# Two chunks of attention per PE run, half loads of the first k and q, dummy matmuls in early gaps

## The chip, the cores and the metric

The kernel runs on one core of one Trainium2 chip. The metric is the device time of one execution in microseconds (us). Before the change the median of three runs is 304.57 us (304.15 to 305.27). In the text PE is TensorE (matmuls), ACT is ScalarE, DVE is VectorE, POOL is GpSimd, and SP is SyncE, whose queue issues all DMA transfers.

## What is computed

Sliding-window causal attention (8 batches, 8 heads, 576 tokens, head size 64, window 64), and then a feed-forward layer with a squared ReLU on all 4608 tokens (512 to 2048 to 512 features):

```python
scores = scale * np.matmul(q, k.transpose(0, 1, 3, 2))
rel = pos[:, None] - pos[None, :]
mask = (rel >= 0) & (rel < window)          # window = 64
attn = softmax(np.where(mask, scores, -1e9))
x = np.matmul(attn, v)                      # per token, heads side by side: (4608, 512)
h = np.maximum(x @ w_in, 0.0)               # (4608, 2048)
out = (h * h) @ w_out                       # (4608, 512)
```

## The kernel before

**Tiling.** The tokens are cut into 36 chunks of 128, and four chunks make a group (9 groups). Groups 0 to 6 and 8 take the first 512 tokens of a batch each; group 7 (LEFT) gathers the last 64 tokens of all eight batches. A chunk's attention is 16 score matmuls (4 head pairs, 2 blocks of 64 queries, 2 heads; contraction over 64 rows), two exps on ACT, two masks on DVE, two halves of values (8 matmuls of 64 columns each) and two normalisations on DVE. The four chunks of a group then share the feed-forward layer.

**Order.** There is no loop that sets the order. A long string, PROGRAM (L16), names one step after another, and each step issues its instructions; every engine runs its own in that order. A step's name, its numbers and, after @, its engine are to be read so:

- lk, lq, dk, dq, dv, li, lo: loads of k and q of a whole group, of k, q or v of one chunk, of a quarter of w_in and w_out (SP).
- ck, cq, ek, eq, cv, ci, co: casts to fp16. cs, cn: copies that shift v by 64 tokens (POOL).
- Tk, Tq: transposes of a group's k or q on PE into PSUM; tk, tq copy them out. Kk, Kq: the same by a DMA transpose (SP). X, x: a chunk's attention output transposed on PE and copied; xx: two chunks by a DMA transpose.
- S, E, M, V, N: scores, exps (E chunk.head), masks, values (V chunk.half) and norms.
- U, R, Q: up projection of one chunk by a quarter of w_in (16 matmuls of 128 columns), its relu on ACT and its square. u, r, s: the same for a whole group and 128 features (4 matmuls of 512 columns).
- O, Z, z: down projection of group 0 as it stands, the copy from PSUM, and the store.
- p, sa, ta, va, vc, vz: down projection of groups 1 to 8 by seven products of half size (Strassen's scheme in Winograd's form): p group.product.half is 8 matmuls of 256 columns, sa and ta are sums on DVE of h and of w_out, va and vc combine products on DVE (one on ACT), vz stores a quarter.
- W: dummy matmuls of zeros at the very start.

Group 0 works in chunks (U, O), groups 1 to 3 use U or u, and from group 1's products (p1.1.0) on, the up blocks of the next group, the products of this one and the attention of the one after are interleaved on PE.

**Buffers.** [...]two for up blocks (ps_up, L151), two for products (ps_out), four for attention (ps_att, L153: transposes, scores and values). A chunk's scores take two banks, its values two. hrelu (hrp, L148) has four buffers. k, q and weight loads share two tags of two buffers each (kq_a and kq_b, L140).

**Squares.** L157 and L158 say on which engine each square runs: all of the groups' on ACT, and of the chunks' some on DVE.

Of the kernel before, what the change touches and what calls it, by code (L numbers as in the profile page):

```python
# [16 lines left out]
    lk0 lq0 dv0 ck0.0@A ck0.1@D ck0.2@P dv2 ck0.3@D W14 Tk0.0 Tk0.1 tk0.0@A dv1 tk0.1@D cq0.2@A  # L17
    cq0.3@P cq0.0@D li0 cq0.1@A Tq0.1 Tq0.0 cv0@A tq0.1@D tq0.0@A cn0@P cv2@A S0 li1 S1 cn2@P
    E0.0 E0.1 cv1@D cs2@P E1.0 M0.0 S2 cs1@P E1.1 M0.1 M1.0 E2.0 cn1@P V0.1 dv3 V0.0 M1.1 E2.1
    N0.1 V1.0 V1.1 N0.0 ci0.0@A ci0.1@P li2 N1.0 S3 N1.1 X0 E3.0 M2.0 X1 E3.1 x0@D x1@D U0.0@u  # L20
    M3.0 ci1.0@A ci1.1@P M3.1 li3 U1.0@u M2.1 R0.0 V2.1 cv3@A V2.0 N2.1 U1.1@o Q0.0 cs3@P N2.0
    R1.0 U0.1@o R1.1 lo1 Q1.0 X2 Q1.1 V3.0 R0.1 V3.1 ci2.0@P x2@D ci2.1@A N3.0 U2.0@u N3.1
    U1.2@u Q0.1 lk1 R2.0 X3 Q2.0 U2.1@o x3@D ci3.0@P ci3.1@A U3.0@u R2.1 R1.2 U0.3@o lo0 Q2.1
    R3.0 Q1.2 U3.1@o R0.3 co1.0@P co1.1@D Q3.0 U0.2@u Q0.3 R3.1 U3.2@u lq1 R0.2 Q3.1 U1.3@o R3.2
    Q0.2 ck1.0@P ck1.1@A U2.3@o ck1.2@D ck1.3@P R1.3 Q3.2 Tk1.0 Q1.3 lo2 Tk1.1 tk1.0@D R2.3
    U3.3@o tk1.1@A co0.0@P U2.2@u co0.1@D Q2.3 R3.3 O0.0.0 R2.2 lo3 Q3.3 O0.0.1 Q2.2 cq1.0@A
    cq1.1@P cq1.2@D O0.1.0 cq1.3@D Tq1.0 Tq1.1 dv4 tq1.0@A O0.1.1 tq1.1@D co2.0@A co2.1@P dv5
    ta1.1@D S6 S4 ta1.0@D E6.0 O0.1.2 dv6 E4.0 ta3.0@D E4.1 O0.0.2 M4.0 E6.1 co3.0@P lk2 M4.1
    co3.1@A S5 M6.0 S7 M6.1 E5.0 cv4@P O0.0.3 ta2.0@D E7.0 E7.1 M5.0 cn4@P V4.0 O0.1.3 M7.0 E5.1
    cv5@P dv7 M7.1 Z0.0 V4.1 M5.1 Z0.1 cs5@P O0.2.0 N4.0 lq2 cv6@P N4.1 V5.0 V5.1 ta2.1@D cn5@P  # L30
    O0.2.1 N5.0 cn6@P O0.2.2 N5.1 cs6@P ta3.1@D O0.3.0 ck2.0@A ck2.1@P z0.0 ck2.2@A ck2.3@D V6.1
    xx5 ta4.0@D V6.0 Tk2.0 cv7@P N6.1 O0.2.3 tk2.0@A N6.0 cs7@P z0.1 O0.3.1 ta4.1@D Z0.2 dv8
    V7.1 O0.3.2 N7.1 cq2.0@A cq2.1@P cq2.2@D V7.0 z0.2 cq2.3@A O0.3.3 N7.0 dv9 Tq2.0 Z0.3 Tq2.1
    tq2.0@D U4.0@u tq2.1@A z0.3 U4.3@u xx7 R4.0 Tk2.1 Q4.0 cv8@P R4.3 tk2.1@D U4.1@u dv10 Q4.3
    cn8@P R4.1 U4.2@u dv11 Q4.1 cv9@P S9 R4.2 U5.2@u cn9@P E9.0 dk12 Q4.2 E9.1 cs9@P S8 M9.0
    R5.2 U5.1@u M9.1 E8.0 dk13 Q5.2 V9.0 E8.1 S10 R5.1 M8.0 U6.3@u cv10@P M8.1 E10.0 dk14 N9.0
    E10.1 V8.0 cs10@P M10.0 Q5.1 V9.1 V8.1 M10.1 cv11@P R6.3 dk15 U5.3@u N8.0 cn10@P Q6.3 N9.1
    V10.0 R5.3 cs11@P V10.1 N8.1 dq12 U5.0@u N10.0 Q5.3 ek12@P S11 N10.1 R5.0 ek13@P xx9 U7.0@u
    E11.0 E11.1 M11.0 ek14@P Q5.0 M11.1 dq13 R7.0 U7.3@u Q7.0 ek15@P V11.1 R7.3 dq14 V11.0 N11.1
    U6.1@u Q7.3 N11.0 eq12@P p1.1.0 R6.1 xx11 U6.0@u Q6.1 U6.2@u R6.0 dq15 p1.1.1 Q6.0 eq13@P  # L40
# [36 lines left out]
    N25.1 E26.1 dl30 M26.0 p4.6.0 ek39@P s5.8 M26.1 r5.9 p4.6.1 dl31 s5.9 eq28@P u5.10 va4.1 Kk9
    p4.7.0 r5.10 u5.11 s5.10 eq29@P V25.0 r5.11 dv36 S27 N25.0 p4.7.1 eq30@P E27.0 E27.1 V26.0
    M27.0 xx25 p4.5.0 s5.11 N26.0 eq31@P M27.1 V26.1 u5.4 va4.2 Kq7 N26.1 V27.1 r5.4 u5.5 N27.1
    s5.4 V27.0 p4.5.1 r5.5 N27.0 dv37 cv36@P s5.5 u5.7 sa5.1.0@D xx27 u5.6 va4.3 r5.7 sa5.2.0@D  # L80
    p4.4.0 s5.7 r5.6 vc4.3 dk40 p4.4.1 s5.6 p4.3.0 vc4.2 vz4.3 u5.13 vz4.2 cv37@P u5.12 dk41
    r5.13 p4.3.1 s5.13 r5.12 dk42 p5.1.0 sa5.3.0@D s5.12 u5.14 sa5.3.1@D ek40@P dk43 sa5.4.0@D
    u5.15 r5.14 vc4.1 dv38 S28 s5.14 p5.1.1 r5.15 E28.0 ek41@P u6.1 vz4.1 E28.1 M28.0 s5.15 dv39
    S29 M28.1 r6.1 ek42@P u6.0 sa5.1.1@D E29.0 E29.1 dv42 V28.1 sa5.2.1@D p5.2.0 r6.0 ek43@P
    M29.0 s6.1 p5.2.1 M29.1 Kk10 s6.0 sa5.4.1@D cv38@P va5.0 u6.2 N28.1 u6.8 vc5.0 r6.2 dv43
    V28.0 s6.2 p5.6.0 cv39@P N28.0 r6.8 u6.3 vz5.0 s6.8 cv42@P dv40 u6.9 r6.3 p5.6.1 s6.3 dv41
    r6.9 V29.1 va5.1 S30 s6.9 u6.10 E30.0 N29.1 dk32 E30.1 cv43@P V29.0 M30.0 S31 r6.10 N29.0
    u6.11 E31.0 dk33 M30.1 E31.1 p5.7.0 M31.0 r6.11 M31.1 cv40@P xx29 s6.10 p5.7.1 s6.11 u6.4
    va5.2 cv41@P dk34 V31.0 r6.4 V30.0 N31.0 u6.5 ek32@P s6.4 N30.0 dk35 p5.5.0 r6.5 ek33@P
# [25 lines left out]
def kernel(  # L115
# [38 lines left out]

    NV = 8
    LEFT = B - 1
    SQUARE = "AAAA"  # L157
    SQUARE4 = ('ADDA', 'AADA')  # L158
    FQ = DFF // 4

# [550 lines left out]
```

The softmax here doesn't subtract the row's maximum and nothing guards it: scores larger than these inputs give would overflow.

## Time and profile before

| what | before |
|---|---|
| median of 3 runs | 304.57 us |
| profiled execution | 303.55 us |
| its span, first to last instruction | 301.8 us |
| PE busy | 287.6 us |
| ACT busy | 220.7 us |
| DVE busy | 187.1 us |
| POOL busy | 107.8 us |
| first matmul of U0.0 | 19.31 us |
| first matmul of p1.1.0 | 74.93 us |
| start of the last matmul's tail (p8.3.1) | 297.8 us |

The time of an execution holds 1.75 us around the span. An engine's busy time is the sum of its instructions. Matmuls are pipelined, so that one begins before the one before it has ended; the distance from one start to the next is what a block costs, and the busy share alone doesn't tell how well PE is used. Steps were put to times by counting: PE's matmuls come in the order of the string, and the number of each step is known.

### The profile page before, as it was taken

Reading aid. Unit: us, or ns where it says so; the run is one execution under the profiler, and the core shown is the slowest. Engines: PE = TensorE matmul, PEld = TensorE weight load, DVE = VectorE, ACT = ScalarE, POOL = GpSimd, SP = SyncE. Lnnn points to the kernel's source line nnn. Section 1 sums busy time; section 2 is a strip of 40 time slices with the busy share of each in tenths; the row PEclk is TensorE's granted clock in tenths of the full one; section 3 lists DMA queues with packets and bytes.
Section 4 is the critical chain, followed back from the end, with each engine's and each line's share of the span. In section 5 each row is a group of like instructions: output and inputs, shape, how many; then the busy total and the mean of one; then the engine's idle time right before and its main releaser. Section 6 shows DMA issues by size and latency. Waiting matters only on the chain.

```text
span 301.8 us, 7861 instructions
## 1 busy us (share of the span) xinstructions
PE 287.6 (95%) x3198; PEld 196.4 (65%) x3198; DVE 187.1 (62%) x395; ACT 220.7 (73%) x386; POOL 107.8 (36%) x161
## 2 busy tenths in 40 slices
PE   7489997999999999999999999999999999999994
PEld 2379953698865666666656666656667566666683
DVE  3676679868559666755855585555766296524453
ACT  2879975699799679578886785688865887877710
POOL 3444229556246408522832662133440350000000
PEclk9759999999999999999999999999999999999999
DMA  7999999999999999999999978999979905210323
GB/s 233 300 361 371 350 269 281 273 194 189 196 214 231 205 198 259 199 203 242 205 182 219 224 191 169 181 270 213 230 168 226 212 3 74 102 35 2 70 72 104
DMA packets 159523, 59.75 MB, mean 198 GB/s; under 512 B 140544, under 2 KB 154880, under 8 KB 159488
## 3 DMA queue, kind: packets, MB, share of 16 engines
q1 hardware_dynamic: 159488, 59.26, 89.3%
q8 instruction: 25, 0.41, 0.6%
q14 instruction: 10, 0.08, 0.1%
HBM read 38.80 MB, written 9.44 MB: 160 GB/s over the span
## 4 chain that ended last, share of the span: by engine, by line
PE 80%; DVE 6%; DMA 6%; ACT 3%; SPq 2%; issue 1%; POOL 1%; ACTq 0%
PE pps L580 32%; PE hps L417 31%; PE hps L408 6%; PE av L365 5%; DMA w_st<-in_moe_w_out_dram 3%; PE ops L464 3%; PE sc L339 2%; DMA st<-in_v_dram 2%; DVE pm L354 2%; ACT hrelu L429 2%; SPq L183 1%; DVE h_sum L540 1%; DVE h L450 1%; ACT h L448 1%; POOL w_out L278 1%
## 5 line engine op out<-in xcount | busy, mean ns | idle before, releaser
L429 ACT ACTIVATE hrelu<-hps 128x512 f32<-128x512 f32 x144 | 85.3, 595 | 47.5 <-PE hps L417 43.4
L417 PE MATMUL hps<-xT,w_in 128*128 128x512 f16 x448 | 110.5, 380 | 0.0
L448 ACT ACTIVATE h<-hrelu 128x512 f16<-128x512 f32 x132 | 82.7, 634 | 3.3
L417 PEld LDWEIGHTS <-w_in 128*128 128x128 f16 x448 | 41.8, 98 | 35.7
L580 PEld LDWEIGHTS <-h_sum 128*128 128x128 f16 x512 | 48.6, 98 | 12.4
L282 POOL CAST v_ev<-st 128x512 f16<-128x512 f32 x36 | 25.5, 708 | 69.2 <-DMA st<-in_v_dram 56.8
L580 PE MATMUL pps<-w_sum,h_sum 128*128 128x256 f16 x384 | 48.2, 273 | 0.0
L540 DVE TENSOR_TENSOR h_sum<-h 128x1024 f16<-128x1024 f16 x32 | 23.2, 745 | 33.5 <-PE pps L580 23.2
L580 PEld LDWEIGHTS <-h 128*128 128x128 f16 x384 | 36.9, 98 | 9.5 <-DVE osp L598 0.5
L348 ACT ACTIVATE pm<-sc 128x512 f16<-128x512 f32 x72 | 38.4, 604 | 2.1 <-PE sc L339 1.9
L354 DVE TENSOR_TENSOR pm<-pm,mask_inner 128x512 f16<-128x512 f16 x56 | 29.4, 550 | 7.0 <-ACT pm L348 6.7
L408 PE MATMUL hps<-xT,w_in 128*128 128x128 f16 x512 | 32.5, 223 | 0.3 <-DVE xT L393 0.2
L580 PE MATMUL pps<-w_out,h 128*128 128x256 f16 x256 | 31.7, 273 | 0.4 <-DVE osp L598 0.4
L376 DVE TENSOR_TENSOR x_sb<-av,rden 128x256 f16<-128x256 f32 x72 | 30.5, 424 | 2.5
L408 PEld LDWEIGHTS <-w_in 128*128 128x128 f16 x512 | 30.4, 100 | 0.9 <-issue 0.2
L591 DVE SCALAR_TENSOR_TENSOR ws<-pps,ws 128x512 f32<-128x512 f32 x24 | 16.5, 687 | 21.9 <-PE pps L580 21.9
L598 DVE SCALAR_TENSOR_TENSOR osp<-pps,ws 128x512 f32<-128x512 f32 x32 | 21.8, 684 | 9.6 <-PE pps L580 9.6
L365 PEld LDWEIGHTS <-pm 128*64 128x64 f16 x576 | 14.0, 112 | 16.7 <-issue 8.5
L271 POOL CAST k<-st 128x512 f16<-128x512 f32 x28 | 18.1, 659 | 15.7 <-DMA st<-in_k_dram 14.9
L271 POOL CAST q<-st 128x512 f16<-128x512 f32 x24 | 14.8, 616 | 21.3 <-DMA st<-in_q_dram 21.1
L375 DVE RECIPROCAL rden<-av 128x4 f32<-128x4 f32 x72 | 12.6, 175 | 13.6 <-PE av L365 13.5
L365 PE MATMUL av<-v_ev,pm 128*64 128x65 f16 x384 | 20.1, 202 | 0.5 <-DVE pm L354 0.4
(62 smaller groups left out, 257.8 us busy)
## 6 DMA issues: line engine op xcount, KB each, us to landing
st<-in_v_dram SPq DMA_DIRECT2D x40, 256.0 KB, 4.4
st<-in_k_dram SPq DMA_DIRECT2D x28, 256.0 KB, 5.0
out_dram<-osp SPq DMA_DIRECT2D x28, 256.0 KB, 3.1
st<-in_q_dram SPq DMA_DIRECT2D x20, 256.0 KB, 4.7
w_st<-in_moe_w_in_dram SPq DMA_DIRECT2D x4, 1024.0 KB, 10.1
w_st<-in_moe_w_out_dram SPq DMA_DIRECT2D x4, 1024.0 KB, 8.4
kq_st<-in_k_dram SPq DMA_DIRECT2D x3, 1024.0 KB, 7.6
kq_st<-in_q_dram SPq DMA_DIRECT2D x3, 1024.0 KB, 9.0
```

What stands on the lines that cost most here:

```text
L271: copier(e)(out=kq16(key, i // 4)[:, :, i % 4, :].rearrange("p a (b d) -> p a b d", d=D), in_=st[key, i][:].rearrange("p (a b) d -> p a b ...
L282: copier(e)(out=v_evs[slot(i)][:, :, 0:D], in_=st["v", i][:])
L348: nc.scalar.activation(out=pm[:], in_=live["s", i][hh][:], func=AF.Exp, scale=1.0 / float(D) ** 0.5)
L354: nc.vector.tensor_tensor(out=pms[i, hh][:], in0=pms[i, hh][:], in1=mask[:], op=ALU.min)
L365: nc.tensor.matmul(av[64 * blk:64 * blk + 64, h % 4, 0:65], pms[i, h % 2][:, h // 2, blk, :], vv[:, h, 0:65], start=True, stop=True)
L376: nc.vector.tensor_tensor(out=xs[i // 2][:, 2 * half:2 * half + 2, i % 2, :].rearrange("p c (b d) -> p c b d", d=D), in0=av[:, :, 0:D].rea ...
L408: nc.tensor.matmul(hps[:, f, :], w_in_q[fq][:, c, f * P:(f + 1) * P], xT_of(i // 4)[:, i % 4 // 2, c, a:a + P], start=(c == 0), stop=(c == ...
L417: nc.tensor.matmul(hps[:], w_in_q[f // 4][:, c, f % 4 * P:(f % 4 + 1) * P], xT_of(g)[:, :, c, :], start=(c == 0), stop=(c == DMC - 1))
L429: nc.scalar.activation(out=hrelu[:] if key == "U" else hrelu[:].rearrange("p (f t) -> p f t", t=P), in_=hps[:], func=AF.Relu, scale=H_SCAL ...
L448: nc.scalar.activation(out=out, in_=hr, func=AF.Square)
L540: eng.tensor_tensor(out=out, in0=in0, in1=in1, op=op)
L580: nc.tensor.matmul(live["p", g, k][:, m, :], lhs, rhs, start=(f == 0), stop=(f == 7))
```

## The change

- From group 2 on (chunk 8 and later), SS j issues the scores of chunks 2j and 2j+1 back to back, and VV j all four halves of their values. The steps before that, S and V, stay for chunks 0 to 7, and the string is ordered anew throughout.
- k and q of group 0 come in two loads each (tokens 0 to 255, then 256 to 511), and casts, transposes and copies of that group go by token halves. In chunks 0 and 1, scores, exps and masks go by halves of the heads.
- w n issues n dummy matmuls of 128 columns; seven such steps (67 matmuls) stand before U0.0, and W14 becomes W13.
- q of group 2 is transposed by DMA (Kq2) and not on PE (Tq2); the scores of that group read q with a stride (Q_RUN).
- Of the groups' squares, those of even feature blocks in groups 2 and 3, and of every fourth block in groups 4 to 8, move from ACT to POOL (36 of 112); of the squares of chunks 0 to 3, one in four moves from DVE to POOL.
- Group 0's down projection runs with three accumulators, one of them in ps_up (O_UP), ordered by quarters of w_out.
- The last output quarter (group 8) is combined and stored in two halves (vh, vy).
- In the start some casts and copies run on another engine than before.

The diff, with the string cut to its beginning, the part around group 2 and 3, and its end:

```diff
 PROGRAM = """
-    lk0 lq0 dv0 ck0.0@A ck0.1@D ck0.2@P dv2 ck0.3@D W14 Tk0.0 Tk0.1 tk0.0@A dv1 tk0.1@D cq0.2@A
-    cq0.3@P cq0.0@D li0 cq0.1@A Tq0.1 Tq0.0 cv0@A tq0.1@D tq0.0@A cn0@P cv2@A S0 li1 S1 cn2@P
-    E0.0 E0.1 cv1@D cs2@P E1.0 M0.0 S2 cs1@P E1.1 M0.1 M1.0 E2.0 cn1@P V0.1 dv3 V0.0 M1.1 E2.1
-    N0.1 V1.0 V1.1 N0.0 ci0.0@A ci0.1@P li2 N1.0 S3 N1.1 X0 E3.0 M2.0 X1 E3.1 x0@D x1@D U0.0@u
...
-    vc8.3 vz8.3 p8.3.0 vc8.2 p8.3.1 vz8.2 vc8.1 vz8.1
+    lq0.0 lk0.0 dv0 li0 cq0.0@A cq0.1@D W13 Tq0.0 tq0.0@A ck0.0@D ck0.1@P lk0.1 w11 Tk0.0 cv0@A
+    tk0.0@D lq0.1 cn0@P w16 S0.1 li1 S0.0 E0.0.1 S1.0 E0.0.0 S1.1 M0.0.1 E0.1.0 M0.0.0 E0.1.1
+    ci0.0@P ci0.1@D E1.0.1 E1.1.1 E1.0.0 M0.1.0 M0.1.1 E1.1.0 w16 V0.0 M1.0.1 ck0.2@A ck0.3@P
+    V0.1 M1.1.1 dv1 M1.0.0 M1.1.0 w5 Tk0.1 N0.0 cq0.2@A cq0.3@P tk0.1@D dv3 w9 Tq0.1 N0.1
+    tq0.1@A li3 w7 X0 x0@A w3 S2 ci1.0@D ci1.1@P S3 E2.0 U0.0@u E2.1 M2.0 E3.0 cv1@P U0.1@o M2.1
+    dv2 E3.1 M3.0 cs1@P R0.0 M3.1 cv3@A cn1@P li2 V1.1 V1.0 Q0.0 N1.1 cs3@P R0.1 N1.0 Q0.1 X1
...
+    cv9@P U4.3@u z0.3 Q4.1 cs9@P xx7 R4.3 U4.2@u cv10@P Q4.3 cn9@P R4.2 U5.2@u dv11 cs10@P Q4.2
+    cn10@P SS4 R5.2 dk12 U5.1@u Q5.2 E8.0 E8.1 U5.3@u M8.0 dk13 E9.0 M8.1 E9.1 M9.0 R5.1 SS5
+    M9.1 dk14 R5.3 Q5.1 cv11@P E10.0 U6.3@u dk15 E10.1 M10.0 cs11@P E11.0 M10.1 E11.1 ek12@P
+    dq12 M11.0 Q5.3 VV4 M11.1 R6.3 ek13@P U6.0@u dq13 N8.0 Q6.3 N8.1 U7.3@u R6.0 N9.0 ek14@P
...
+    SS7 vz1.3 r2.11 s2.10 dq18 p1.4.1 s2.11 E14.0 ek19@P p1.3.0 vc1.2 E14.1 dq19 E15.0 u2.4
+    M14.0 eq16@P E15.1 M14.1 u2.5 M15.0 r2.4 Kk4 M15.1 eq17@P VV6 r2.5 s2.4 p1.3.1 s2.5 N12.0
+    N12.1 vz1.2 u2.6 eq18@P N13.0 dv16 N13.1 u2.7 r2.6 sa2.1.0@D eq19@P VV7 r2.7 xx13 sa2.3.0@D
+    s2.6 s2.7 N14.0 N14.1 u2.12 Kq4 N15.0 u2.13 N15.1 r2.12 sa2.2.0@D p2.1.0 s2.12 r2.13 xx15
+    sa2.3.1@D p2.1.1 s2.13 cv16@P sa2.4.0@D u2.14 va2.0 vc1.1 cn16@P dv17 u2.15 r2.14 s2.14
+    vz1.1 r2.15 dv18 s2.15 SS8 sa2.1.1@D p2.2.0 E16.0 dv19 sa2.2.1@D E16.1 u3.0 E17.0 M16.0
...
+    p8.4.0 va8.3 p8.4.1 vc8.3 vz8.3 p8.3.0 vc8.2 p8.3.1 vz8.2 vh8.1.0 vy8.1.0 vh8.1.1 vy8.1.1
 """
...
-    SQUARE = "AAAA"
-    SQUARE4 = ('ADDA', 'AADA')
+    SQUARE = ('PAPA', 'PAAA')
+    SQUARE4 = ('APDA', 'AADA')
+    Q_RUN = (2,)
+    O_UP = ((0, 2),)
...
+        nc.sync.dma_start(
+            out=st[:].rearrange("p h (n c) -> p n h c", n=2)[:, n],
+            in_=src[g, :, 2 * P * n:2 * P * (n + 1), :].rearrange("h (t r) d -> t h (r d)", r=2))
...
-    def scores(i):
+    def scores(i, half=None):
...
-                    nc.tensor.matmul(
-                        sc[hh][:, hp, blk, :], kT[r0:r0 + 64, hp, a0:a0 + P],
-                        qTs["q", g][r0:r0 + 64, hp, a + 64 * blk:a + 64 * blk + 64],
-                        start=True, stop=True)
+                    r0, t0 = 64 * hh, a + 64 * blk
+                    qT = qTs["q", g][r0:r0 + 64, hp, :]
+                    if g in Q_RUN:
+                        qT = qT.rearrange("d (r p) -> d p r", p=P)[:, t0 // 4:t0 // 4 + 16, :]
+                    else:
+                        qT = qT[:, t0:t0 + 64]
+                    nc.tensor.matmul(
+                        sc[hh][:, hp, blk, :], kT[r0:r0 + 64, hp, a0:a0 + P], qT,
+                        start=True, stop=True)
...
-        return SQUARE[b % 4] if key == "U" else SQUARE4[a // 4][b]
+        return SQUARE[a > 3][b % 4] if key == "U" else SQUARE4[a // 4][b]
...
+    def warm_short(n):
+
+        ps = ps_out.tile([P, P], FP32, name="warm", tag="ps_o")
+        for _ in range(n):
+            nc.tensor.matmul(ps[:], zeros[:, 0:P], zeros[:, 0:P], start=True, stop=True)
...
-            live["o", g, ts] = ps_out.tile([P, DM], FP32, name="ops", tag="ps_o")
+            pool, tag = (ps_up, "ps_u") if (g, ts) in O_UP else (ps_out, "ps_o")
+            live["o", g, ts] = pool.tile([P, DM], FP32, name="ops", tag=tag)
...
+    def whole_half(g, c, m):
+
+        t = live["c", g, c, m] = opool.tile([P, HALF], FP32, name="osh", tag="osb")
+        nc.vector.scalar_tensor_tensor(
+            out=t[:], in0=live["p", g, (2, 3, 4, 5)[c]][:, m], scalar=OUT_SCALE,
+            in1=live["w", g, (0, 3, 2, 2)[c]][:, m], op0=ALU.mult, op1=ALU.add)
...
+        "SS": lambda j: [scores(i) for i in (2 * j, 2 * j + 1)],
+        "VV": lambda j: [values(i, half) for i in (2 * j, 2 * j + 1) for half in range(2)],
```

## Prediction

> **What bounds the kernel now.** I read the page from the top (busy shares, slices), then the waits of PE, then PE's timeline in order of time. The page first:
>
> ```profile
> span 301.8 us, 7861 instructions
> ...
> PE 287.6 (95%) x3198; PEld 196.4 (65%) x3198; DVE 187.1 (62%) x395; ACT 220.7 (73%) x386; POOL 107.8 (36%) x161
> ...
> PE   7489997999999999999999999999999999999994
> ...
> PEclk9759999999999999999999999999999999999999
> DMA  7999999999999999999999978999979905210323
> ```
>
> PE is full from slice 3 on; only the first three slices (22 us), slice 6 and the last have holes. The clock is low in slices 1 and 2. DMA is full for the first 45 us, so early PE work is paced by arrivals. The stretch from the first Strassen product (p1.1.0 starts at 74.93) to the last matmul:
>
> ```profile
> core 0: us, PE busy (x) PEld busy (x) DVE busy (x) ACT busy (x) POOL busy (x), PEclk, DMA share, GB/s
> 74.93:297.85 222.92, 222.18 (x2179) 146.84 (x2176) 134.10 (x266) 163.45 (x290) 70.75 (x105) 1.00 0.85 171
> ```
>
> PE idles 0.7 us of 222.9 there, ACT is at 73%: taking work off ACT alone is worth nothing. The end is set by the sum of PE's issue times. What that sum holds beside arithmetic is in PE's timeline (start, duration, matmuls; ends are modelled, so I read start to start):
>
> ```profile
> 135.95 1.04 PE L580 MATMUL pps<-w_out,h_sum 128*128 128x256 f16 x8
> 136.82 1.89 PE L417 MATMUL hps<-xT,w_in 128*128 128x512 f16 x8
> 138.55 0.71 PE L580 MATMUL pps<-w_out,h 128*128 128x256 f16 x5
> ...
> 146.04 0.64 PE L339 MATMUL sc<-qT,kT 64*128 64x64 f16 x32
> 146.61 1.04 PE L417 MATMUL hps<-xT,w_in 128*128 128x512 f16 x4
> 147.66 0.32 PE L365 MATMUL av<-v_ev,pm 128*64 128x65 f16 x8
> 147.91 1.05 PE L580 MATMUL pps<-w_sum,h_sum 128*128 128x256 f16 x8
> 148.88 0.32 PE L365 MATMUL av<-v_ev,pm 128*64 128x65 f16 x8
> ...
> 154.32 1.04 PE L580 MATMUL pps<-w_sum,h_sum 128*128 128x256 f16 x8
> 155.29 0.41 PE L339 MATMUL sc<-qT,kT 64*128 64x64 f16 x16
> 155.63 1.90 PE L417 MATMUL hps<-xT,w_in 128*128 128x512 f16 x8
> ```
>
> A product block takes 0.87 (135.95 to 136.82), an up block 0.865. Ahead of a scores or values run the block takes 0.97 (154.32 to 155.29; 147.91 to 148.88): 0.10 lost per excursion. Scores of 16 matmuls take 0.34 and of 32 take 0.57, so 16 cost 0.23 and the run 0.11. Eight values take 0.25, sixteen 0.38 (152.19 to 152.57), so eight cost 0.13 and the run 0.12. Scores next to values each keep their 0.115. So an excursion to the 64-row or 64-column shape and back costs 0.10, plus 0.115 for each run in it.
>
> The sum proves it: 112 products of 0.873 + 112 ups of 0.866 + 4 U chunks of 0.89 + 24 scores of 0.23 + 48 halves of values of 0.13 + 56 runs of 0.115 + 49 excursions of 0.10 = 97.8 + 97.0 + 3.6 + 5.5 + 6.2 + 6.4 + 4.9 = 221.4; measured 222.9, so 1.5 is stalls.
>
> [...]
>
> **Part 1: double runs.** Counting PE's steps in both program texts (merging neighbours): before 77 runs in 67 excursions, after 39 in 39. From p1.1.0 on: 56 in 49 against 24 in 24. Saved there: 32 x 0.115 + 25 x 0.10 = 6.2. The 0.9 or so before p1.1.0 is in part 2's sum.
> What it adds is a wait. Scores of two chunks take four banks of ps_att, values of two chunks take four, and the pool has four. VV needs all four exps of the preceding SS (4 x 0.51 = 2.04, from six in 3.04 at 13.02), and the next SS needs all four norms (4 x 0.60: 0.175 + 0.42). Between SS and the next double run lie 3 to 20 blocks. Worst in group 2: from the end of U5.2 ACT owes R5.2, four exps, R5.1, R5.3, Q5.1, four exps = 0.52 + 2.04 + 1.04 + 0.53 + 2.04 = 6.2, while PE has SS4, U5.1, U5.3, SS5, U6.3 = 4.1 and VV4 of 0.6: PE loses 1.6. Elsewhere it fits: SS7 to VV6 has 3.5 us of blocks for 3.1 of ACT after the run; VV6 to VV7 2.6 us for norms of 2.4 started inside the run.
> A second new wait: x of chunks 14 and 15 is ready only after VV7's four norms, and SP has xx13, dv16 and Kq4 ahead of xx15. Counted from VV7's end: xx13 leaves SP at 1.3 (issue 1.84, as at 96.92), Kq4 at 3.5 to 4.8 (issue 2.2 to 3.5), xx15 lands 4.0 later, 7.5 to 8.8; u3.0 is due at six blocks + SS8 + one block = 6.9. Loss 0.6 to 1.9, I take 1.0. With 1.0 for the rest: 2.0 of stalls.
> Sum from p1.1.0: 97.8 + 97.0 + 5.5 + 6.2 + 24 x 0.215 + 2.0 = 213.7 (no U chunk is left in it), against 222.9.
>
> **Part 2: the start.** Before, the chain of waits runs through the issue of v loads on SP, the landing of dv1 at 13.0, masks, norms, and U0.0 at 19.31. After, half loads of q and k come first. From k0 and q0 landing at 6.3 and 9.5 (1 MB in 3.2) I take 0.5 MB in 1.6 to 2.0: q half at about 4.7, k half 6.4, v0 7.5, w_in0 10.5, the other halves 12.3 and 14.2, w_in1 17, v1 and v3 19, w_in3 22, w_in2 26. The first halves come through early: k cast 0.87, transposes 0.6, copy 1.22, so scores at 9.1 (12.40 before), then exps and masks of chunks 0 and 1 in halves (eight for four) to about 13. U0.0 stands on PE behind S2 and S3, which need the second halves: second q half 14.2, cast 0.87, transposes 0.5, copy on ACT 1.0, S2 and S3 0.7, so about 17.5; X0 and its copy end near 17 as well. I take 18.0, range 17 to 20. The w dummies (67 of 128 columns, 0.06 each at full clock, 0.11 at half, so 4 to 7 us in all) stand in the waits; PE is in order, so 16 of them at half clock outlast the 1.22 copy of kT by 0.5 once or twice. In return U blocks run at full clock.
> Then PE meets w_in3 and w_in2: U1.2 needs w_in2's cast (26 + 1.05) and ends at 28.4. Left to p1.1.0: 25 U of 0.895, 6 transposes groups of 0.45, 16 O of 0.87, 8 scores of 0.23, 16 halves of values of 0.13, 10 excursions of 0.215 = 22.4 + 2.7 + 13.9 + 1.8 + 2.1 + 2.2 = 45.1, and the 1.6 of VV4 and 0.2 for the transpose below: p1.1.0 at 75.3. That is with all 32 U blocks done; before, 28 were done at 74.93, so the like time is 78.5. Gain about 3.2; it includes the 1.7 that PE waited for w_out (O0.0.3 at 46.87): ordering O by weight quarter, with a third accumulator in ps_up, puts O0.0.3 at about 49, and w_out3 lands near 45 with 2.1 of casts on POOL.
> Tq2 leaves PE (0.9, in the 45.1); Kq2 goes through SP and DMA instead, 4.4 to 7.2 to landing (kT and qT transposes in the trace). q2's load waits in kq_b for w_out3's casts near 47, lands some 5 later, its casts end near 54; SS4 is due 13 us of blocks after O0.0.3, near 61. Little slack: price 0 to 3, I take 0.2. Group 2's q is then read with a stride by the 64 matmuls of SS4 and SS5; nothing shows its price: 0 if the stride is free, 1.1 if both runs took twice their 0.57, and I take 0.
>
> **Part 3: squares on POOL.** 36 of 112 up squares go from ACT to POOL (8 each in groups 2 and 3, 4 each in 4 to 8) and 4 chunk squares from DVE. ACT loses 36 x 0.634 = 22.8, worth nothing alone; it pays for the exps' punctuality. No POOL multiply is in the trace. Floor: the POOL cast of this size, 0.71. [...] hrelu has four buffers, so a square may be some 3.5 us late before a relu and then PE wait. Taken as 0, at most 3. Casts that change engines in the start stand beside arrivals and count with them.
>
> **Part 4: the end.** PE's last matmul starts its tail at 297.85; 3.95 remain. Halved: DVE about 0.42 for 0.69, the last store 128 KB for 256 (2.4 for 3.1 to landing in the list of issues). I take 0.7 off: 3.25.
>
> **Sum.** 75.3 + 213.7 + 0.2 (the last matmul's tail) + 3.25 = 292.5 of span, against 301.8. The profiled execution took 303.55, that is 1.75 around the span: 294.2. The median shown, 304.57, lies 1.0 above the profiled execution: 295.2.
>
> **Rivals.**
> A, the forecast, 295.2, own range 292 to 299: 0.60.
> B, the steady saving comes but the start gives nothing, because arrivals pace it with or without halves, and transposes in SP's queue cost a microsecond in several groups. For: DMA is at 9 until 45 us. Against: the 1.7 and the half clock are real holes. 295.2 + 3.2 + 2 = 300.4: 0.18.
> C, the change doesn't do what it says[...]. Against: two chunks' scores at 146.04 took 0.57, not 0.68. Then only what lies outside is left, 303 to 306, within 0.5%: 0.07.
> D, slower: the four banks. Every double run takes the whole pool, so PE waits for the fourth exp or norm each time, and ACT's queue (relu, square, exps) sets the pace. It decides from a mean wait of 0.43: 28 x 0.43 = 12.0 less 2.6 counted = 9.4, all of the gain. At 0.55 it gives 295.2 + 12.8 = 308. For: group 2's worked 1.6. Against: blocks between the runs, and 22.8 off ACT: 0.15.
>
> Measurement tells 0.5% (303.0 to 306.1 is no change). Faster 0.78, same 0.07, slower 0.15. The range 291 to 304 holds A, B and a part of C.
>
> **What shows it.** PE's timeline: SS runs of 0.57 and VV runs of 0.64 between starts (32 matmuls each), blocks at 0.87 between; from p1.1.0 to the last matmul 214; p1.1.0 near 75; clock without the 5. Waits of PE on the exps' line or on x_sb norms above 10 us in all would show D; a first U later than 20 shows part 2 wrong; waits of PE's relu buffers on POOL show part 3 wrong.

## The result, and the profile after

| what | before | forecast | after |
|---|---|---|---|
| median, us | 304.36 (the three runs above and a fourth) | 295.2 | 314.82 (four runs, 313.94 to 315.10) |
| profiled execution, us | 303.55 | 294.2 | 315.10 |
| span, us | 301.8 | 292.5 | 313.4 |

The changed kernel takes 1.0334 times as long (95% interval 1.0303 to 1.0364). It is slower; the forecast was 3% faster.

The page of the changed kernel (first the shares, then 40 slices of 7.8 us, counted from 0):

```profile
PE 289.6 (92%) x3248; PEld 200.9 (64%) x3248; DVE 196.2 (63%) x395; ACT 200.9 (64%) x353; POOL 151.2 (48%) x201
...
PE   7757986799999999999959999999999999999995
...
PEclk9997999599999999999997999999999999999999
```

PE's busy time has grown by only 2 us, but the span by 11.6: PE stands more. There are deeper holes than before in slices 2, 3, 6 and 7 and a new one in slice 20 (5 where it was 9), and the clock falls in slices 3, 7 and 21, which is once in the start and twice just behind a hole. Cut at the steps that the prediction named (end of U1.2, start of p1.1.0, end of the last matmul), the windows of the changed kernel are these; the last cut lies 0.1 behind the end of the last matmul, which is 309.60:

```profile
core 0: us, PE busy (x) PEld busy (x) DVE busy (x) ACT busy (x) POOL busy (x), PEclk, DMA share, GB/s
0.00:33.03 33.03, 23.92 (x371) 18.76 (x372) 18.70 (x57) 19.98 (x36) 14.64 (x26) 0.95 1.01 301
33.03:90.67 57.64, 51.36 (x769) 39.03 (x766) 37.47 (x74) 40.74 (x73) 27.16 (x36) 0.94 0.88 224
90.67:309.70 219.03, 214.31 (x2116) 143.16 (x2112) 139.33 (x264) 140.21 (x246) 109.35 (x139) 0.99 0.85 169
309.70:313.40 3.70, 0.00 (x0) 0.00 (x0) 0.70 (x2) 0.00 (x0) 0.00 (x0) 0.79 0.38 125
```

| stretch | forecast | measured | over |
|---|---|---|---|
| start to the end of U1.2 | 28.4 | 33.0 | 4.6 |
| to p1.1.0 | 46.9 | 57.6 | 10.7 |
| to the end of the last matmul | 213.9 | 219.0 | 5.1 |
| tail | 3.25 | 3.70 | 0.5 |

So 20.9 us are missing, half of them in the second stretch, which is a fifth of the time. PE's four largest waits over the whole changed kernel (what waits, what it waits for, us in total, times, longest):

```profile
PE av L401 <- DVE pm L390: 5.5, 4, 2.6
PE pps L623 <- DVE osp L641: 3.3, 1, 3.3
PE xt_ps L423 <- DVE x_sb L412: 2.9, 3, 1.7
PE sc L374 <- ACT qT L327: 1.4, 1, 1.4
```

Of the first, 3.9 lie in the second stretch, at V4.0; the wait of 3.3 is at p3.7.0 in the third. Three of the four are waits for DVE, which is busy for 63% of the span: a mean share says nothing of one queue at one moment. PE's timeline around the two largest of them, and around SS4 and SS5:

```profile
55.13 0.22 PE L401 MATMUL av<-v_ev,pm 128*64 128x65 f16 x2 [2.65 <-DVE pm L390]
56.63 0.60 PE L401 MATMUL av<-v_ev,pm 128*64 128x65 f16 x14 [1.28 <-DVE pm L390]
57.16 5.30 PE L507 MATMUL ops<-w_out,h 128*128 128x512 f16 x12
...
74.11 1.94 PE L374 MATMUL sc<-qT,kT 64*128 64x64 f16 x32
75.99 1.96 PE L444 MATMUL hps<-xT,w_in 128*128 128x128 f16 x32
...
164.34 1.20 PE L623 MATMUL pps<-w_sum,h_sum 128*128 128x256 f16 x8 [3.26 <-DVE osp L641]
165.33 3.46 PE L453 MATMUL hps<-xT,w_in 128*128 128x512 f16 x8
168.62 1.04 PE L623 MATMUL pps<-w_sum,h_sum 128*128 128x256 f16 x8
```

Three things are seen here. V4 waits 2.65 and then 1.28 for masks. The O blocks behind it take 5.30 for three, and the two up blocks behind p3.7.0 take 3.29 from start to start, where two take 1.73 elsewhere: the clock has been halved after each hole (the granted clock is 0.50 from 55.85 to 62.68 and from 165.08 to 168.49). And SS4 takes 1.88 from start to start, where the prediction had 0.57.

DVE's timeline ahead of the first hole shows why the masks are late:

```profile
50.46 1.09 DVE L583 TENSOR_TENSOR w_sum<-w_out 128x1024 f16<-128x1024 f16 x1
...
52.49 1.09 DVE L583 TENSOR_TENSOR w_sum<-w_out,w_sum 128x1024 f16<-128x1024 f16 x1
53.51 0.83 DVE L390 TENSOR_TENSOR pm<-pm,mask_inner 128x512 f16<-128x512 f16 x1
54.26 0.82 DVE L390 TENSOR_TENSOR pm<-pm,mask_first 128x512 f16<-128x512 f16 x1
...
55.75 0.82 DVE L390 TENSOR_TENSOR pm<-pm,mask_first 128x512 f16<-128x512 f16 x1
...
58.68 0.68 DVE L583 TENSOR_TENSOR w_sum<-w_out,w_sum 128x1024 f16<-128x1024 f16 x1
```

The second mask_first (to 56.57) releases PE at 56.63. Three sums of w_out (ta1.0, ta3.0, ta2.0, from 50.46) stand in DVE's queue ahead of four masks (from 53.51), and both kinds take longer than elsewhere: a sum takes 0.68 at 58.68 and 1.09 at 50.46, and a mask 0.83 here for 0.42 in the median of those with no POOL work beside them. POOL is casting v and k and shifting v meanwhile. Over the whole changed kernel the 25 masks of full size with no POOL work beside them take 0.41 to 0.43. Of the 14 that lie wholly beside POOL work six take 0.78 to 0.83, seven take 1.25 to 1.26, and one takes 0.41. The long ones run for about 0.98 beside one POOL instruction of 1.04 or more (a square, or a cast of w), the six for about 0.55 beside a shorter cast or copy. So the longer the POOL instruction that a mask meets, the longer the mask. Five of the eight masks of 1.25 or more in the whole kernel meet a square; before the change no mask took over 0.85. The normalisation x_sb, whose large input comes from PSUM, takes 0.42 with POOL work or without.

The second hole, in DVE's timeline of the changed kernel:

```profile
154.98 1.07 DVE L583 TENSOR_TENSOR h_sum<-h 128x1024 f16<-128x1024 f16 x1 [2.97 <-POOL h L481]
155.97 0.83 DVE L390 TENSOR_TENSOR pm<-pm,mask_inner 128x512 f16<-128x512 f16 x1
...
157.73 2.75 DVE L390 TENSOR_TENSOR pm<-pm,mask_inner 128x512 f16<-128x512 f16 x3
...
163.61 0.68 DVE L641 SCALAR_TENSOR_TENSOR osp<-pps,ws 128x512 f32<-128x512 f32 x1
```

DVE first stands for 2.97, because the sum needs a square that is now on POOL (s3.14, behind v casts there). Then it works off three sums and four masks at the slow rate and four norms, and vc3.0, which frees the bank that p3.7.0 needs, comes last in this queue, at 163.61.

### The profile page after: what moved, and what is told of

Read it like the earlier page. It is cut to its first block, busy times and chain, and to the rows that moved or that the text cites. A ratio compares the mean times of both kernels' runs of the same rounds, so it can differ in the third digit from the quotient of the medians.

```text
span 313.4 us, 8024 instructions
## 1 busy us (share of the span) xinstructions
PE 289.6 (92%) x3248; PEld 200.9 (64%) x3248; DVE 196.2 (63%) x395; ACT 200.9 (64%) x353; POOL 151.2 (48%) x201
## 4 chain that ended last, share of the span: by engine, by line
PE 70%; DVE 12%; DMA 9%; SPq 3%; ACT 2%; POOL 1%; issue 1%; DVEq 0%; POOLq 0%; ACTq 0%
PE pps L623 28%; PE hps L453 27%; PE hps L444 6%; DVE pm L390 6%; DMA w_st<-in_moe_w_in_dram 4%; PE ops L507 3%; PE av L401 3%; DVE h_sum L583 3%; DMA w_st<-in_moe_w_out_dram 3%; PE sc L374 2%; DMA st<-in_v_dram 2%; DVE x_sb L412 2%; DMA qT<-q 1%; DVE w_sum L583 1%; SPq L201 1%
## 5 line engine op out<-in xcount | busy, mean ns | idle before, releaser
L453 PE MATMUL hps<-xT,w_in 128*128 128x512 f16 x448 | 109.4, 383 | 0.2 <-DMA xT<-x_sb 0.2
L481 POOL TENSOR_TENSOR h<-hrelu 128x512 f16<-128x512 f32 x40 | 43.7, 1096 | 63.2 <-ACT hrelu L465 55.7
L453 PEld LDWEIGHTS <-w_in 128*128 128x128 f16 x448 | 43.0, 99 | 40.4 <-issue 2.3
L484 ACT ACTIVATE h<-hrelu 128x512 f16<-128x512 f32 x96 | 60.6, 631 | 2.7
L623 PEld LDWEIGHTS <-h_sum 128*128 128x128 f16 x512 | 49.6, 98 | 17.5 <-issue 3.9
L583 DVE TENSOR_TENSOR h_sum<-h 128x1024 f16<-128x1024 f16 x32 | 25.6, 810 | 26.9 <-PE pps L623 18.3
L390 DVE TENSOR_TENSOR pm<-pm,mask_inner 128x512 f16<-128x512 f16 (+1 forms) x58 | 35.6, 648 | 10.0 <-ACT pm L382 9.4
L382 ACT ACTIVATE pm<-sc 128x512 f16<-128x512 f32 (+1 forms) x76 | 37.2, 581 | 2.8 <-PE sc L374 2.8
L444 PEld LDWEIGHTS <-w_in 128*128 128x128 f16 x512 | 30.7, 101 | 3.9 <-issue 2.1
L286 POOL CAST k<-st 128x512 f16<-128x512 f32 x28 | 20.6, 758 | 13.2 <-DMA st<-in_k_dram 13.0
L286 POOL CAST q<-st 128x512 f16<-128x512 f32 x24 | 15.4, 657 | 18.4 <-DMA st<-in_q_dram 18.2
L401 PEld LDWEIGHTS <-pm 128*64 128x64 f16 x576 | 11.7, 112 | 12.4 <-DVE pm L390 6.4
```

The lines of the kernel that those rows point to most:

```text
L286: copier(e)(out=kq16(key, i // 4)[:, :, i % 4, :].rearrange("p a (b d) -> p a b d", d=D), in_=st[key, i][:].rearrange("p (a b) d -> p a b ...
L382: nc.scalar.activation(out=pms[i, hh][:, hs], in_=live["s", i][hh][:, hs], func=AF.Exp, scale=1.0 / float(D) ** 0.5)
L390: nc.vector.tensor_tensor(out=pms[i, hh][:, hs], in0=pms[i, hh][:, hs], in1=mask[:, hs], op=ALU.min)
L444: nc.tensor.matmul(hps[:, f, :], w_in_q[fq][:, c, f * P:(f + 1) * P], xT_of(i // 4)[:, i % 4 // 2, c, a:a + P], start=(c == 0), stop=(c == ...
L453: nc.tensor.matmul(hps[:], w_in_q[f // 4][:, c, f % 4 * P:(f % 4 + 1) * P], xT_of(g)[:, :, c, :], start=(c == 0), stop=(c == DMC - 1))
L481: nc.gpsimd.tensor_tensor(out=out, in0=hr, in1=hr, op=ALU.mult)
```

## Experiments

Two theories stand against each other. Theory 1: single places carry the loss after the start (V4.0 and vc3.0 above all), each hole is paid twice, once as a wait and once as a half clock, and the squares on POOL feed the second. Theory 2, the rival: no single place carries it, so that a mended hole opens again elsewhere, and an edit alone brings little. Beside both stands what the start costs by itself. Each ratio below is to executions of the kernel before made beside that run, whose median was 304.8 to 305.4; the changed kernel was not run again beside them, so that a difference of medians to it holds to about 1 us. Times of steps are from one profiled execution each.

**1. All squares back off POOL.** The table of squares is near that of before: none on POOL.

```diff
-    SQUARE = ('PAPA', 'PAAA')
-    SQUARE4 = ('APDA', 'AADA')
+    SQUARE = ('AAAA', 'AAAA')
+    SQUARE4 = ('ADDA', 'AADA')
```

> The changed kernel with all up squares back on ACT (and the chunk squares as before on ACT and DVE); nothing else differs. Theory 1 (the squares on POOL make DVE late: they come late in POOL's queue, and while POOL runs a two-input DVE operation takes twice as long, masks 0.82 us for 0.41): the wait of 3.3 us ahead of p3.7.0 goes, and the half clock of 3.4 us after it; from p1.1.0 to the last matmul 218.9 falls to 213 to 215, total 309 to 311. Theory 2 (the order is to blame, POOL is not): the wait stays, and ACT has 23 us more to do; total 314 to 318.

Measured: 311.83, ratio to before 1.0217 (1.0186 to 1.0247), 3.0 less than the changed kernel and between the two expectations. p1.1.0 is at 90.78, as in the changed kernel, and the end of the last matmul at 306.39: this stretch takes 215.6 instead of 218.9, so the squares cost 3.3 there. Most of that lies at one place: the wait at p3.7.0 falls from 3.26 to 2.19, no half clock follows, and the two up blocks behind it take 1.73 from start to start again (3.29 in the changed kernel). That is 2.8 of the 3.3.

**2. q of group 2 turned on PE, read without a stride.**

```diff
-    O0.1.3 dv10 tk2.1@A O0.3.3 Z0.1 Kq2 U4.0@u
+    O0.1.3 dv10 tk2.1@A O0.3.3 Z0.1 Tq2.0 Tq2.1 tq2.0@D tq2.1@A U4.0@u
...
-    Q_RUN = (2,)
+    Q_RUN = ()
```

> The changed kernel with q of group 2 transposed on PE again (Tq2 and two copies in the place of Kq2), and read without a stride. Theory 1 (a strided read of q halves the matmul's rate): SS4 and SS5 take 0.6 to 0.7 us from start to start for 1.9, so 2.5 us less, against 0.9 us of transposes added: total 312.5 to 313.8. Theory 2 (these runs wait for banks, exps or the transfer): they stay at 1.9 us or the wait shows ahead of them, total 315 to 316.5.

PE's timeline of this kernel:

```profile
76.14 0.64 PE L371 MATMUL sc<-qT,kT 64*128 64x64 f16 x32
```

Without the stride SS4 and SS5 take 0.64 each for 1.94, so the stride costs 2 x 1.3 = 2.6 on PE. Yet the kernel took 316.12, ratio 1.0334 (1.0286 to 1.0381), as the changed one. From SS4 to p1.1.0 it takes 15.4 for 16.6: about 1.4 of the 2.6 comes back at VV4, which now waits before it starts and several times within, for exps and masks among others, and takes 1.73 from start to start for 0.65. So the slow strided scores had hidden most of the wait that the prediction expected at VV4. Ahead of SS4, which starts at 76.14 for 74.11, the transposes on PE cost 0.9, and this execution was 0.8 later already at the end of U1.2. The stride's price on PE is shown; that its removal in this form brings anything is not.

**3 and 4. Before's order up to p1.1.0, the changed order after it.** The first 366 steps are those of before; then come the U blocks of group 1 that before does later (U6.0, U7.1, U7.2), and from there on the changed string goes on. 3 keeps the changed squares in groups 2 to 8, 4 has all of the groups' squares on ACT.

```diff
+    ... V11.0 N11.1 U6.1@u Q7.3 N11.0 eq12@P
+    U6.0@u R6.0 Q6.0 U7.1@u Kk3 U7.2@u R7.1 eq13@P Q7.1 R7.2 xx11 eq14@P Q7.2
     dq15 U6.2@u R6.1 sa1.3.0@D Q6.1 dv12 p1.1.0 R6.2 sa1.1.1@D p1.1.1
```

> The steps of the kernel before up to p1.1.0, then what the changed kernel's string had done more by then, then its string from p1.1.0 on, with its double runs and its squares on POOL. Theory 1 (the start loses 12 us, the rest is about even): p1.1.0 of this string near 79, then 219 as in the changed kernel, 301.5 of span, total 302.5 to 305. Theory 2 (the double runs themselves cost the time, the start is innocent): 310 or more.

> The same with all squares where they were before (ACT). So the double runs from group 3 on and the split last store stand alone against the kernel before. Theory 1 (double runs save 5 to 6 us[...], POOL's squares gave that back): 297 to 299.5. Theory 2 (the double runs wait for four exps or norms each, squares are innocent): 303 or more, and no difference from the run with squares on POOL.

Measured: 306.97, ratio 1.0073 (1.0035 to 1.0111), and 304.8, ratio 0.9995 (0.9969 to 1.0021). Both missed: the first was expected at 302.5 to 305, the second at 297 to 299.5. Part of the miss is of my making: U blocks back to back at the seam wait 2.5 for relus on ACT, and p1.1.0 starts at 83.1 and 82.8 for 78.5. The other part is the wait at p3.7.0, still 2.5 and 2.0. Still, with the changed squares and the changed rest, before's order up to p1.1.0 alone takes 7.9 off the changed kernel.

**5. vc3.0 moved ahead,** right behind p3.2.1, which computes its last input.

```diff
-    p3.2.1 sa3.4.1@D s4.0 ... r4.8 ek26@P dq26 vc3.0 p3.6.1
+    p3.2.1 vc3.0 sa3.4.1@D s4.0 ... r4.8 ek26@P dq26 p3.6.1
```

> The changed kernel with one step moved: vc3.0 stands in DVE's order right after p3.2.1, ahead of one h_sum and four norms. Theory 1 (p3.7.0 waits for its bank only because vc3.0 is queued behind them, and the hole then halves the clock): p3.7.0 follows p3.6.1 within 0.5 us, no half clock at 165 to 168.5, total 309 to 311. Theory 2 (DVE is behind by more than that step, so the lost time comes back at VV11 or u5.0): total 313 to 315.

PE's timeline of this kernel:

```profile
161.13 2.13 PE L620 MATMUL pps<-w_sum,h_sum 128*128 128x256 f16 x16
163.10 1.89 PE L450 MATMUL hps<-xT,w_in 128*128 128x512 f16 x8
```

The wait is gone (p3.6.1 and p3.7.0 run as one row of 16) and the blocks behind it keep the full clock: 310.69, ratio 1.0193 (1.0149 to 1.0237), as theory 1 has it. At the place itself, from p3.6.1 to p3.7.1, 4.9 are gained: 3.2 of the hole and 1.7 of the half clock. The whole stretch from p1.1.0 to the end of the last matmul takes 217.1 for 218.9, so only 1.8 less, but that is no proof of theory 2. The profiled execution was the slowest of the four (312.55; the others 310.50 to 310.87), and 1.6 of what it lost was lost ahead of the step that was moved, at SS8 (a transfer of q, 1.2 for 0.5) and at u4.0 (1.1 for 0.2):

```profile
PE sc L371 <- DMA qT<-q: 1.2, 1, 1.2
PE hps L450 <- ACT pm L379: 1.1, 1, 1.1
```

Another 1.2 was lost behind it, at p4.2.0 and u5.9; whether the edit or this execution did that is open.

**6. The three sums of w_out behind N4.1.**

```diff
-    M6.1 cn5@P ta1.0@D S4 cn4@P lk2 ta3.0@D S7 E4.0 O0.1.1 ta2.0@D E7.0
+    M6.1 cn5@P S4 cn4@P lk2 S7 E4.0 O0.1.1 E7.0
...
-    N4.0 cs7@P O0.2.2 N4.1 cn6@P
+    N4.0 cs7@P O0.2.2 N4.1 ta1.0@D ta3.0@D ta2.0@D cn6@P
```

> The changed kernel with three sums of w_out (ta1.0, ta3.0, ta2.0, 1.09 us each on DVE) moved from between the masks of chunks 4 to 7 to behind the norms of chunk 4. Theory 1 (DVE's queue makes V4.0 late, and the hole of PE halves the clock for the next 6.8 us): V4.0 starts before 53.5 instead of 55.1, no half clock from 56 to 62.7, p1.1.0 at 84.5 to 86.5, total 308.5 to 311. Theory 2 (the time comes back at SS4, VV4 or VV5, since ACT and DVE are as late there): p1.1.0 stays above 89, total 313 to 315.

Measured: 311.16, ratio 1.0178 (1.0118 to 1.0239). V4.0 starts at 53.04 for 55.13, the half clock from 55.85 to 62.68 is gone, and p1.1.0 is at 86.81 for 90.67: 3.9 gained from moving three DVE instructions that have nothing to do with attention. V4.0 still waits 1.3 for its second mask, and 1.1 of the gain goes again at Tk2.1, which now waits for a cast of k behind the sums in DVE's queue. What the slow masks add to the wait at V4.0, beside the sums, was not tested by itself.

**7. Dummies in the two holes,** 44 ahead of V4.0 and 50 ahead of p3.7.0, in a bank of ps_up. This keeps the waits and takes the half clock away. It is the test of "paid twice".

```diff
+    def warm_up(n):
+
+        ps = ps_up.tile([P, P], FP32, name="warm", tag="ps_u")
+        for _ in range(n):
+            nc.tensor.matmul(ps[:], zeros[:, 0:P], zeros[:, 0:P], start=True, stop=True)
...
-    V5.0 V4.0
+    V5.0 wu44 V4.0
...
-    s4.8 r4.9 xx21 p3.7.0
+    s4.8 r4.9 xx21 wu50 p3.7.0
```

> The changed kernel with dummy matmuls of 128 columns in the two holes of PE: 44 ahead of V4.0 and 50 ahead of p3.7.0 (2.4 and 2.8 us at full clock, so within the holes). No wait is removed. Theory 1 (a hole costs twice, as a wait and then as a half clock): the half clock from 55.9 to 62.7 and from 165 to 168.5 goes, O0.1.2, O0.2.2 and O0.0.3 take 0.87 us each for 1.7 to 1.9, total 309.5 to 311.5. Theory 2 (these blocks are slow for another reason): total 314 to 316.

The same window in the changed kernel and in this one, each from its windows:

```profile
55.85:62.68 6.83, 6.05 (x36) 2.39 (x38) 4.65 (x13) 0.18 (x1) 1.75 (x3) 0.50 0.26 57
```

```profile
55.85:62.68 6.83, 5.41 (x66) 3.01 (x67) 6.62 (x20) 1.67 (x4) 1.85 (x3) 1.00 0.34 69
```

PE's timeline of the kernel with dummies:

```profile
57.84 2.76 PE L510 MATMUL ops<-w_out,h 128*128 128x512 f16 x12
```

The clock is 1.00 for 0.50, and the twelve O matmuls take 2.76 for 5.30. V4.0 and p3.7.0 start no earlier than the DVE lets them (55.99 and 162.54), but the kernel takes 310.65, ratio 1.0173 (1.0133 to 1.0213), 4.2 less. So the half clocks alone cost about 4 us. The two low stretches of the changed kernel last 6.83 (55.85 to 62.68) and 3.41 (165.08 to 168.49).

**8 and 9. Before's order further, then the changed rest with vc3.0 early and all of the groups' squares on ACT.** 8 changes over ahead of u2.0, 9 after u2.3 (its seam is shown).

```diff
+    ... p1.6.0 r2.2 dv14 sa1.4.1@D s2.2 cv12@P u2.3 vc1.0 cn12@P dv15
     cv13@P p1.6.1 vz1.0 r2.3 p1.7.0 dk16 s2.3 va1.1 cs13@P u2.8 cv14@P dk17
```

> The kernel before, its steps up to u2.0 in its own order, then the rest in the changed kernel's order, squares on ACT, and vc3.0 right after p3.2.1. So the U blocks keep the products between them at the seam. Theory 1 (double runs from group 3 on save[...], once no step is late): u2.0 near 81.3, 211 from there to the end of PE's work, span 296, total 297 to 299. Theory 2 (double runs give the saving back in waits elsewhere): 302 to 305.

> As the run with the old start and vc3.0 early, but the order of before is kept up to u2.8, so that the sums for p1.6 come as early as there. Theory 1 (the hole ahead of p1.6.0 and the half clock of 3.4 us after it were a fault of the seam, 3.8 us in all; double runs save the rest): 298.5 to 300.5. Theory 2 (the saving is lost elsewhere): 302 to 304.

Measured: 8 took 302.99, ratio 0.9917 (0.9888 to 0.9946), against 297 to 299 of theory 1 and within the 302 to 305 of theory 2: at its seam PE waits 2.1 for a sum of h ahead of p1.6.0 and runs at half clock from 87.74 to 91.16. 9, with the seam where PE has work on both sides, took **300.34, ratio 0.9822 (0.9792 to 0.9853)**, which beats both kernels. In its profiled execution, the slowest of the eight (302.44), PE still waits 3.5 for masks, the longest 1.9 ahead of a half clock from 52.70 to 56.11, and 2.3 for the transfer of q at SS8. The first is in before's order, though before itself waits only 0.6 for masks. The second is the prediction's Kq4, but at SS8 (q not there yet), not at xx15 behind it.

**10. Values and x of chunk 1 ahead of w_in's second quarter,** to see whether the order of the start makes U1 late: dv1 before li1, cv1 and cs1 earlier, and V1, N1, X1 and U1.0 moved ahead.

```diff
-    cn0@P w16 S0.1 li1 S0.0 ... V0.1 M1.1.1 dv1 M1.0.0
+    cn0@P w16 S0.1 dv1 li1 S0.0 ... V0.1 M1.1.1 M1.0.0
...
-    X0 x0@A w3 S2 ci1.0@D ci1.1@P S3 E2.0 U0.0@u E2.1 M2.0 E3.0 cv1@P U0.1@o M2.1
+    X0 x0@A V1.1 V1.0 N1.1 N1.0 w3 S2 ci1.0@D ci1.1@P E2.0 U0.0@u E2.1 X1 x1@A S3 U1.0@u M2.0 E3.0
+    U0.1@o M2.1
```

> The changed kernel with v of chunk 1 loaded ahead of w_in1, its cast and shift ahead of POOL's cast of w_in1, values and norms of chunk 1 ahead of S2, and U1.0 ahead of U0.1. Theory 1 (the start is late because chunk 1's x waits for v1 behind w_in1, and then behind four masks on DVE): U1.0 starts at 19.5 to 21 for 24.6, no half clock from 25 to 28.5, U1.2 ends at 29.5 to 31.5 for 33.0, total 312 to 313.5. Theory 2 (arrivals of w_in3 and w_in2 pace the start in any order): U1.2 ends at 32.5 or later, total 314 to 315.5.

Measured: 314.01, ratio 1.029 (1.025 to 1.033). U1.0 starts at 22.24 for 24.62, but U1.2 ends only at 32.13 for 33.03. p1.1.0 gains 2.3, but in the profiled execution nothing is left of it at the last matmul (309.80 for 309.60): 1.3 are lost ahead of p3.6.1, and the rest behind p3.7.0, where the half clock lasts 6.8 instead of 3.4. The time fits the second expectation (314 to 315.5), the end of U1.2 neither (by 31.5, or at 32.5 or later). Inconclusive on the start.

**11. Three mends together:** squares on ACT (1), vc3.0 early (5), sums late (6), each as above.

> The changed kernel with squares on ACT, vc3.0 early and the three sums of w_out late. If the three losses are apart from each other: 3.0, 4.1 and 3.7 us less, 314.8 falls to 304. If they share the same holes (theory 2: what DVE gains in one place it waits for in another): 307 to 309.

The stretch from p1.1.0 in this kernel's windows:

```profile
86.81:300.50 213.69, 212.57 (x2115) 142.96 (x2112) 129.64 (x264) 157.42 (x282) 68.38 (x103) 1.00 0.86 173
```

Measured: 306.31, ratio 1.004 (1.0022 to 1.0058), between the 304 of losses that are apart and the 307 to 309 of losses that share their holes. PE idles 1.1 of 213.7 here, as little as before the change. The stretch gains 5.4, and 5.1 of it at p3.7.0 and its half clock. The squares alone gave 3.3 (1), 2.8 of it at the same place, and vc3.0 gave 4.9 there (5). So these two mends don't add up: each takes away a part of one hole, and moving vc3.0 takes away all of it. What stays is the time ahead of p1.1.0: 86.81 against the 78.5 of before for the same work.

**12. The 67 short dummies of the start removed.**

```diff
-    ck0.0@D ck0.1@P lk0.1 w11 Tk0.0 cv0@A ... cn0@P w16 S0.1
+    ck0.0@D ck0.1@P lk0.1 Tk0.0 cv0@A ... cn0@P S0.1
```

> The changed kernel without the 67 short dummy matmuls ahead of U0.0 (W13 stays). Theory 1 (they keep PE's clock at full through the start, and the U blocks gain from it): half clock before U0.0, the first U blocks at 1.6 us instead of 0.9, total 316 to 317.5. Theory 2 (the start waits for arrivals, POOL and DVE, and PE's speed there is hidden): U1.0 and U1.2 start where they did (24.6 and 32.0, within 0.7), total 314 to 315.5.

PE's timeline of this kernel, and then the same 48 matmuls in the changed one:

```profile
18.02 3.60 PE L441 MATMUL hps<-xT,w_in 128*128 128x128 f16 x32
...
24.34 2.84 PE L441 MATMUL hps<-xT,w_in 128*128 128x128 f16 x48 [0.67 <-ACT xT L426]
```

```profile
24.62 4.47 PE L444 MATMUL hps<-xT,w_in 128*128 128x128 f16 x48 [0.67 <-ACT xT L429]
```

Measured: 313.29, ratio 1.0275 (1.023 to 1.0319), 1.5 less than with them, and less than either theory expected (316 to 317.5, 314 to 315.5). Here U0.0 runs at half clock (12.49 to 22.73), and U1.0, U1.1 and U0.3 take 2.84. With the dummies the clock is full until 25.13 and half from there to 28.55, so that the same 48 matmuls take 4.47. The dummies shorten the half clock but don't remove it, and they move it to where more work is. U1.2 ends at 31.13 for 33.03. In all seven runs with the changed start in its order a half clock of 3.4 or 6.8 lies on the blocks from U1.0 on, and U1.2 ends at 32.8 to 33.8.

## Why the prediction was wrong

**The sum from p1.1.0 on was right.** The forecast was 213.7, and experiment 11 measures 213.6 to the end of the last matmul. Its terms are in the changed kernel too: scores of two chunks take 0.573 from start to start and values 0.637 (medians of 12 each), a product 0.873, and a block ahead of such a run 0.96 to 0.97. The double runs do save what was said, and the border of two chunks shows no loss (0.573, where two single runs of 0.34 would make 0.68), so C falls. The 2.0 for stalls fits experiment 11 (about 2.2 by difference), though not by its reason: u3.0 does not wait for xx15, and Kq4 costs 0.5 at SS8. What the sum left out in the changed kernel is below, under the squares and vc3.0. The 0.2 added for the last matmul's tail was counted already, since the 222.9 of before ends with the last matmul (297.83).

**The step that failed first: "p1.1.0 at 75.3".** It was at 90.67. It was worked out as a sum of PE's blocks plus one stall of 1.6 for VV4 (ACT's queue) and 0.2 for Kq2, and DVE's queue was not followed at all. In the 10.7 over, from the end of U1.2 on:
- V4 waits 3.9 for masks that stand behind ta1.0, ta3.0 and ta2.0, and the half clock behind it takes about 2.5 in the O blocks. Moving the sums gave 3.9 back (6), and filling the hole kept the clock (7).
- The stride of q in group 2, "and I take 0", costs 2.6 (2). Its upper end, 1.1, was too low too: it allowed twice the time of a run, and the run takes three times as long.
- S6 waits 1.45 for the copy of q on ACT, and U6.1 waits 0.8 for a square on DVE. Neither was tried.
- Against these stands the 1.6 for VV4, which did not come, because the strided scores gave ACT time: without the stride about 1.4 of it comes (2). About 1 us stays without a place.

**The start: 4.6 late at U1.2.** U0.0 at 18.0 was right (17.63), and the first halves of q and k land at 5.01 and 6.85 for 4.7 and 6.4, so the half loads do what was said. The error is between U0.0 and U1.2, where the prediction let arrivals set the pace: 10.4 forecast, 15.4 measured. In the trace PE waits there 0.95 for the casts of w_in1 (landed at 18.26 for 17), 0.53 for the shift of v on POOL, 1.69 and 0.91 for norms on DVE (masks hold up only the first, by about 0.5), and 0.67 for the copy of x on ACT, and it loses about 1.6 to the half clock of 25.13 to 28.55. These chains of casts, values, norms and copies behind an arrival had not been counted. The arrivals were late too: w_in2 landed at 28.13 for 26, and with a cast of 1.05 and a block of 1.05 behind it (an estimate from the trace's durations) U1.2 could not have ended before 30.2 behind that landing, in any order of PE. Of all this only the clock was tested (12: 1.9 earlier without dummies). "In return U blocks run at full clock" was wrong: before, the first two U blocks took 1.65 each from start to start at the half clock (0.50 from 11.32 to 21.56) and later ones 0.89, and here U1.0, U1.1 and U0.3 meet a half clock again (25.13 to 28.55). How much of the rest the order of the start can give back stays open after experiment 10.

**Squares on POOL, "taken as 0, at most 3", cost 3.3** in the stretch from p1.1.0 (1 against the changed kernel), 2.8 of it at p3.7.0. A square on POOL takes 1.096 (mean of 40), for the 0.71 of a cast that was taken as the floor. What was missed is what they do to others: a sum on DVE waits 2.97 for one of them, and masks and sums, whose two inputs are both in SBUF, slow down beside them (a mask to 1.26 from 0.42, a sum to as much as 1.55 from 0.68). ACT's relief had been counted as worth nothing, and that holds: 11 has ACT busy for 217.9 us and PE still full.

**vc3.0**'s place in DVE's queue costs 4.9 (5), and the 2.8 of the squares are a part of that: with the squares back on ACT a wait of 2.19 is left, with vc3.0 moved none. The prediction looked for waits on the four banks of attention. The bank that was late is one of the two of products. **The tail** was to shrink by 0.7 and shrank by 0.2 (4.0 to 3.8, from the end of the last matmul, 297.83 and 309.60): halving the store did little.

**The rivals.** D, slower, had the right sign and the wrong mechanism: its mark, waits of PE on exps or norms above 10 us, isn't there; waits on norms are 2.9 in all, and those on exps are none. B was right not to trust the start, but the start costs more than it brings. Its reason, arrivals, holds in part: by the estimate of 30.2 above, 1.8 of the 4.6 at U1.2 would stay with every other wait gone. No rival had a DVE queue in it, though the trace of before shows DVE at 134 of 222.9 us and POOL's casts beside masks that are sometimes at 0.80.

## What to carry to other kernels

When PE is full, every step that is moved on another engine has to be followed in that engine's queue up to the PE instruction that waits for it; a sum of PE's own blocks is a lower bound and not a forecast. A hole in PE of 3 us should be priced at its length plus what the half clock behind it takes (1.7 for the 3.41 us behind p3.7.0, about 2.5 for the 6.83 behind V4.0), so that 0.2 us saved at forty places is lost with two such holes. Take the half that saves and keep the half that worked: here before's start with the new rest, vc3.0 early and the squares on ACT is 1.8% faster than before, while the whole change is 3.3% slower. And a mend that gains at one place should be read at that place: the sum of a stretch in one execution also holds waits that have nothing to do with it (experiment 5).

## What the hardware showed that was not expected

- A DVE mask with two SBUF inputs takes 0.42 us alone, about 0.83 beside POOL casts and copies (medians 0.61 to 0.67), and 1.25 where it meets a square (1.04) or a cast of w on POOL; the sums of h and w_out take 0.68 alone and about 1.09 beside POOL work, up to 1.55 beside a square; x_sb, reading PSUM, takes 0.42 in both cases.
- Reading the moving operand with a stride of 128 fp16 elements makes 32 score matmuls take 1.88 us from start to start instead of 0.57 to 0.64.
- Behind the start, PE holes of 2.6 to 3.3 us brought, in every run that has one (the changed kernel, 1, 2, 5, 6, 10, 12), a half clock of 3.41 or 6.83, which begins within about 1 us of the hole's end. From 1.9 to 2.5 us the length doesn't decide it: 1.88 (9) and 2.08 (8) brought one, 1.98 (4), 2.19 (1), 2.26 (9) and 2.52 (3) brought none.
